# Strassen's seven products for the down projection, with the output projection moved to the last sections

## The chip, the core and the metric

The kernel runs on one core of one Trainium2 chip. The metric is the device time of one execution in microseconds (us), as the median of several runs. The engines are called as in the profile: PE is TensorE (PEld its weight loads), DVE VectorE, ACT ScalarE, POOL GpSimd, SP SyncE, which issues all the DMAs here.

## The reference

One transformer block over 2048 tokens of width 576: attention with 32 heads of width 18, and a gated feed-forward of width 4608 that does not add to it but gates it.

```python
def _A_ref(x, wqkv, wo):
    qkv = (x @ wqkv).reshape(B, S, 3, H, Dh).transpose(2, 0, 3, 1, 4)
    q, k, v = qkv[0], qkv[1], qkv[2]
    scores = jnp.einsum("bhqd,bhkd->bhqk", q, k) * (Dh ** -0.5)
    p = _softmax(scores, axis=-1)
    o = jnp.einsum("bhqk,bhkd->bhqd", p, v)
    return o.transpose(0, 2, 1, 3).reshape(B, S, D) @ wo

def _B_ref(x, w_gate, w_up, w_down):
    return (_gelu(x @ w_gate) * (x @ w_up)) @ w_down

x = A_x
xn = _layernorm(x, axis=-1)
s = _A_ref(xn, A_wqkv, A_wo)
g = _silu(_B_ref(xn, B_w_gate, B_w_up, B_w_down))
return x + s * g
```

All inputs and the output are float32.

## The kernel before

**Precision.** TensorE's operands are in float32r, and every operand is split into a high part (`h`, the value rounded to float32r) and a low part (`l`, the remainder). A product is three matmuls: high by high, high by low, low by high. So each operand made on the chip costs a copy that rounds and a subtraction. For weights and activations POOL does both (`split`, L95), in the lead-in ACT and POOL, in the last sections ACT and DVE (`split_av`).

**Prologue.** Layer norm, transposes and the q, k, v projections run first, and leave q and k (`qk`), v (`vs`) and the transposed tokens (`xhs`) in DRAM.

**Sections.** The rest is a line of 144 feed-forward sections. A section is one block `b` of 512 tokens (four of them) by 128 rows of the width 4608: 27 pairs of matmuls, gate on one half of the array's rows and up on the other (`gate_up`, L387). 36 sections make a block. Two sections (g = 0 and g = 1, even and odd) make a round `r`, 18 rounds to a block. Each section loads the weights of the next and splits them on POOL in three pieces (`wh`, `wl`, five buffers each). Its end is the activation (`activate`, L411): ACT and DVE in turns, six instructions of 512 elements.

**The down product** of a round (`down`, L428) multiplies the two halves of 128 rows that the round made, 512 tokens by 256, with 256 rows of `w_down`, 256 by 576: four blocks of 128 tokens, each 12 matmuls of 288 columns, 48 in all. DVE adds each block to `Y` in SBUF. It runs at the end of the section after the round, an even one, so every second section carries one. The rows of `w_down` are loaded and split again in each of the four blocks.

**Attention** is woven into the 128 sections from the tenth on, four to a unit of 512 queries by four heads. A section has 16 specials spread over its pairs (`spread`, L57), in turn a pair of scores (`score_pair`, whose exponential is on ACT) and a pair for the maxima of the next unit (`max_pair`, whose reduction is on DVE). After the pairs come the products with the values (`values`, L745), then, every fourth section, `max_end` (L716): the maxima of a unit are transposed on TensorE, copied by DVE and stored as rows of that unit's queries; then tasks such as the output projection, then the down product. The nine sections ahead of attention are the lead-in, with maxima alone; seven sections follow it.

**PSUM.** Scores, maxima, values, down and output products share one ring of three buffers (`ring`, L383). Whoever takes a buffer waits until the third user before it has been read.

**The output projection** of the first three blocks is done one group of 128 tokens and 288 columns at a time (14 matmuls), one in every second section of the block after; the last block's groups follow in the last sections.

**Order.** TensorE runs in the order in which the program is written. The other engines' queues are ordered by a scheduler, apart from what `keep_in_program_order` holds fast. Each engine takes its own queue in order.

## Time and profile before

| what | us |
|---|---|
| median of three runs | 2622.2 |
| the three runs | 2620.28 to 2622.35 |
| the profiled execution, its own time | 2619.38 |
| its span in the trace | 2617.6 |

The profile is one execution. The page gives the busy time of each engine, the span in 40 slices, the chain of waits that ended last, and the groups of instructions by line; the trace answers further questions: the chain in order of time, a timeline of each engine, and windows with the busy time of each engine in a stretch. Matmuls are pipelined, so that one lasts longer in the rows than the distance to the next; the chain counts the distance. The clock granted to TensorE was full throughout (1.00).

### The profile page before, as it was taken

The page shows a single profiled execution, that of the slowest core. Times are in us where ns is not written, and L with a number is a line of the kernel's source. Part 1 is how long each engine was busy: PE and PEld are TensorE (multiplying, and loading weights), DVE is VectorE, ACT ScalarE, POOL GpSimd, SP SyncE. Part 2 cuts the span into 40 slices and gives each one's busy share as a digit, 9 for nine tenths or more (in the row PEclk, how much of TensorE's full clock was granted, in tenths as well). Part 3 has the DMA queues.
Part 4 walks back from the last instruction along what each step waited for, and adds up shares of the span by engine and source line. Part 5 has one row for each costly group of instructions (what it writes and reads, how often), then busy time and mean ns, then how long its engine had stood idle before and what let it go on. Part 6 is the DMA issues. An engine that isn't in the chain of part 4 may idle for free.

```text
span 2617.6 us, 54490 instructions
## 1 busy us (share of the span) xinstructions
PE 2592.6 (99%) x20982; PEld 1908.5 (73%) x20982; DVE 1923.2 (73%) x2205; ACT 1400.2 (53%) x1675; POOL 1386.9 (53%) x1507
## 2 busy tenths in 40 slices
PE   9999999999999999999999999999999999999999
PEld 8888766777677666777667677777677777767678
DVE  5326888777887878777787877778887777787445
ACT  3223466555566556555566655555665655565642
POOL 2127554555465455555546555555455755555553
PEclk9999999999999999999999999999999999999999
DMA  8876444434355344444445444445345543544342
GB/s 261 264 241 158 115 104 105 105 93 105 102 132 138 100 108 108 127 113 125 108 112 143 113 125 105 123 107 137 101 111 121 140 112 102 137 108 130 77 115 63
DMA packets 394881, 326.81 MB, mean 125 GB/s; under 512 B 107964, under 2 KB 308668, under 8 KB 394624
## 3 DMA queue, kind: packets, MB, share of 16 engines
q1 hardware_dynamic: 394624, 323.32, 46.4%
q8 instruction: 168, 2.75, 0.5%
q14 instruction: 89, 0.73, 0.1%
HBM read 269.79 MB, written 52.88 MB: 123 GB/s over the span
## 4 chain that ended last, share of the span: by engine, by line
PE 94%; DVE 4%; ACT 1%; issue 0%; DMA 0%; POOL 0%; SPq 0%; POOLq 0%; ACTq 0%
PE pg L401 26%; PE py L435 18%; PE acc L754 14%; PE pe L737 9%; PE pm L705 9%; PE pu L401 8%; PE po L168 7%; PE po L591 2%; DVE mx L706 1%; DVE t L422 1%; PE pgu L401 1%; ACT t L420 1%; DVE m L714 1%; DVE t L415 1%; PE pt L229 0%
## 5 line engine op out<-in xcount | busy, mean ns | idle before, releaser
L738 ACT ACTIVATE pT<-pe 128x1024 f32<-128x1024 f32 x1024 | 1049.5, 1027 | 800.8 <-PE pe L737 771.2
L706 DVE TENSOR_REDUCE mx<-pm 128x2 f32<-128x1024 f32 x1024 | 1217.4, 1226 | 170.0 <-PE pm L705 158.0
L401 PE MATMUL pu<-xd,wh 64*128 64x512 f32 x2520 | 919.7, 395 | 0.0
L401 PE MATMUL pg<-xd,wh 64*128 64x512 f32 x2520 | 918.8, 395 | 0.0
L96 POOL TENSOR_SCALAR wh<-raw 128x384 fp32r<-128x384 f32 x432 | 227.5, 528 | 638.9 <-DMA raw<-in_B_w_up_dram 268.2
L401 PEld LDWEIGHTS pg<-xd,wh 64*128 64x128 f32 x2520 | 464.3, 184 | 92.3 <-issue 22.6
L401 PE MATMUL pg<-xd,wl 64*128 64x512 f32 x1260 | 490.8, 390 | 0.9 <-POOL wl L98 0.9
L401 PE MATMUL pu<-xd,wl 64*128 64x512 f32 x1260 | 491.0, 390 | 0.0
L401 PEld LDWEIGHTS pu<-xd,wh 64*128 64x128 f32 x2520 | 464.3, 184 | 11.1
L754 PE MATMUL acc<-pT,VS 128*32 128x512 f32 x4096 | 466.0, 595 | 0.0
L98 POOL TENSOR_TENSOR wl<-raw,wh 128x384 fp32r<-128x384 f32 x432 | 441.2, 1022 | 33.5
L737 PE MATMUL pe<-q,KS 64*128 64x512 f32 x2048 | 413.5, 392 | 0.0
L705 PE MATMUL pm<-KS,q 64*128 64x512 f32 x2048 | 411.4, 389 | 0.0
L441 DVE TENSOR_TENSOR Y<-py,Y 128x576 f32<-128x576 f32 x272 | 206.0, 758 | 226.7 <-PE py L435 226.3
L435 PE MATMUL py<-dh,hh 128*128 128x288 f32 x1152 | 345.9, 300 | 0.0
L435 PE MATMUL py<-dl,hh 128*128 128x288 f32 x1152 | 339.7, 295 | 0.9 <-POOL dl L103 0.9
L435 PE MATMUL py<-dh,hl 128*128 128x288 f32 x1152 | 339.8, 295 | 0.0
L754 PEld LDWEIGHTS acc<-pT,VS 128*32 128x32 f32 x4096 | 120.4, 109 | 275.4 <-issue 229.5
L737 PEld LDWEIGHTS pe<-q,KS 64*128 64x128 f32 x2048 | 192.3, 184 | 110.9 <-DVE mx L706 29.6
L401 PEld LDWEIGHTS pg<-xd,wl 64*128 64x128 f32 x1260 | 232.3, 184 | 34.3 <-POOL wl L98 1.2
L435 PEld LDWEIGHTS py<-dh,hh 128*128 128x128 f32 x1152 | 216.4, 188 | 39.3 <-issue 37.6
L401 PEld LDWEIGHTS pu<-xd,wl 64*128 64x128 f32 x1260 | 232.3, 184 | 7.1
(138 smaller groups left out, 2989.4 us busy)
## 6 DMA issues: line engine op xcount, KB each, us to landing
KS<-qk SPq DMA_DIRECT2D x1536, 36.0 KB
raw<-in_B_w_gate_dram SPq DMA_DIRECT2D x144, 288.0 KB
raw<-in_B_w_up_dram SPq DMA_DIRECT2D x144, 288.0 KB
raw<-in_B_w_down_dram SPq DMA_DIRECT2D x68, 576.0 KB
VS<-vs SPq DMA_DIRECT2D x128, 152.0 KB
qk<-t SPq DMA_DIRECT2D x72, 256.0 KB
q<-qk SPq DMA_DIRECT2D x384, 36.0 KB
xd<-xhs SPq DMA_DIRECT2D x24, 384.0 KB
```

The lines of the kernel that those rows point to most:

```text
L96: first = nc.gpsimd.tensor_scalar(hi, raw, 1.0, 1.0, op0=ALU.mult, op1=ALU.mult)
L98: keep(nc.gpsimd.tensor_tensor(lo, raw, f(hi), op=ALU.subtract))
L168: nc.tensor.matmul(o, st, m, start=(i == 0), stop=(i == len(terms) - 1))
L401: nc.tensor.matmul(o, w[1 + wp][k][rr, c, :], xd[xp][k][rr, c, :], start=(i == 0), stop=(i == len(terms) - 1))
L435: nc.tensor.matmul(py[:, c, 0:288], h[:, tt], w[:, g, 288 * c:288 * c + 288], start=n == 0, stop=n == len(terms) - 1)
L441: nc.vector.tensor_tensor(yy, py[:, :, 0:288], yy, op=ALU.add)
L591: nc.tensor.matmul(po[:, 0:288], o[x][:, k, :], ow[w][:, k, :], start=(m == 0), stop=(m == len(terms) - 1))
L705: nc.tensor.matmul(pm[:, a], QS[u, r][rr, t * P:(t + 1) * P], KS[(u * NA + c) % KB][r][rr, :], start=True, stop=True)
L706: nc.vector.tensor_reduce(MX[u][:, 2 * r:2 * r + 2, t, c], pm, axis=AX.X, op=ALU.max)
L737: nc.tensor.matmul(pe[:, a], KS[(u * NA + c) % KB][r][rr, t * P:(t + 1) * P], QS[u, r][rr, :], start=True, stop=True)
L738: nc.scalar.activation(PT[u, kt][:, 2 * r:2 * r + 2, :], pe, AF.Exp, scale=SCALE)
L754: nc.tensor.matmul(ACC[u][32 * a:32 * a + 32, :], VS[(u * NA + c) % VB][:, v:v + 32], pt[:, a, :], start=first, stop=last, skip_group_chec ...
```

## The change

It changes three things.

1. The down product of a round, a matrix of 2 by 2 blocks of 256 tokens by 128 rows times one of 128 rows by 288 columns, is done with Strassen's seven products. The seven left factors are the four activations' quarters or sums of two of them (`sums_a`), the seven right factors are sums of quarters of `w_down` (`sums_b`). The products are added up over the rounds in `M`, and combined into the four quarters of the result once at the end of a block (`combine`). The right factors, split, are made once, in block 0, and stored in DRAM (`ts`); in the blocks 1 to 3 `load_t` loads them, 16 KB a partition. `T`, `M` and the left factors `ah`, `al` have one buffer each.
2. The output projection leaves the attention sections. In the seven last sections all 16 groups of 128 tokens are projected, 576 columns each; its weights, heads and reciprocals are loaded there. Its tiles lie in the pool that takes over attention's memory.
3. `max_end` moves from the end of its section into the pairs of the next, behind the fifth special.

The splits change hands: `cut` copies on ACT and subtracts on POOL in the attention sections, on DVE in the lead-in and the last sections.

```diff
+PRODUCTS = ((2, (0, 6)), (5, (1, 3)), (3, (2, 5)), (6, (3, 4)), (0, (4, 2)), (4, (5, 1)), (1, (6, 0)))
+    ts = dram.tile([NR, P, 2 * 7 * DC], F32, name="ts")
...
+    def cut(hi, lo, raw, eng):
+        nc.scalar.activation(hi, raw, AF.Copy)
+        eng.tensor_tensor(lo, raw, f(hi), op=ALU.subtract)
+
+    def sums_a(g, h, eng):
+        ah, al = FF["A"]
+        if g == 0:
+            FF["h0"] = h
+            nc.gpsimd.tensor_tensor(h[:, 2], h[:, 1], h[:, 0], op=ALU.subtract)
+            cut(ah[:, 0:2], al[:, 0:2], h[:, 0:3:2], eng)
+        else:
+            h0 = FF.pop("h0")
+            nc.gpsimd.tensor_tensor(h[:, 4:6], h0[:, 0:2], h[:, 0:2], op=ALU.add)
+            nc.gpsimd.tensor_tensor(h[:, 3], h0[:, 0], h[:, 1], op=ALU.add)
+            nc.gpsimd.tensor_tensor(h[:, 2], h[:, 0], h[:, 1], op=ALU.subtract)
+            cut(ah[:, 2:7], al[:, 2:7], h[:, 1:6], eng)
+
+    def load_t(r):
+        nc.sync.dma_start(f(FF["T"]).rearrange("p i m d -> p (i m d)"), ts[r])
+
+    def sums_b(r, raw, eng):
+        q = raw.rearrange("p g (c d) -> p (g c) d", c=2)
+        t, T = ffn.tile([P, 5, DC], F32, name="tsum"), FF["T"]
+        eng.tensor_tensor(t[:, 1:3], q[:, 0:4:2], q[:, 1:4:2], op=ALU.add)
+        eng.tensor_tensor(t[:, 3:5], q[:, 0:2], q[:, 2:4], op=ALU.subtract)
+        eng.tensor_tensor(t[:, 0], q[:, 0], q[:, 3], op=ALU.add)
+        cut(T[:, 0, 0:2], T[:, 1, 0:2], q[:, 0:4:3], eng)
+        cut(T[:, 0, 2:7], T[:, 1, 2:7], t, eng)
+        nc.sync.dma_start(ts[r], f(T).rearrange("p i m d -> p (i m d)"))
+
+    def down(b, r):
+        (ah, al), T, M = FF["A"], FF["T"], FF["M"]
+        for m, (i, k) in PRODUCTS:
             py = ring("py")
-            for c in range(2):
-                for n, (h, w, g) in enumerate(terms):
-                    nc.tensor.matmul(py[:, c, 0:288], h[:, tt], w[:, g, 288 * c:288 * c + 288],
-                                     start=n == 0, stop=n == len(terms) - 1)
...
+            for t in range(2):
+                tt = slice(t * P, (t + 1) * P)
+                for n, (h, w) in enumerate(((ah, 0), (ah, 1), (al, 0))):
+                    nc.tensor.matmul(py[:, t, 0:DC], h[:, i, tt], T[:, w, k], start=n == 0, stop=n == 2)
             if r == 0:
-                nc.scalar.activation(yy, py[:, :, 0:288], AF.Copy)
+                nc.scalar.activation(M[:, m], py[:, :, 0:DC], AF.Copy)
             else:
-                nc.vector.tensor_tensor(yy, py[:, :, 0:288], yy, op=ALU.add)
+                nc.vector.tensor_tensor(M[:, m], py[:, :, 0:DC], M[:, m], op=ALU.add)
...
+    def combine(one, two):
+        M = FF["M"]
+        one.tensor_tensor(M[:, 6], M[:, 6], M[:, 0], op=ALU.add)
...
+        two.tensor_tensor(M[:, 1], M[:, 1], M[:, 3], op=ALU.subtract)
 
     def gates():
+        for b in FF["gates"]:
+            M = FF["M"]
+            combine(nc.vector, nc.gpsimd)
...
+                tc.keep_in_program_order(nc.scalar.activation(th, y, AF.Tanh, scale=0.25))
+                nc.gpsimd.tensor_scalar(th, th, 1.0, 1.0, op0=ALU.add, op1=ALU.mult)
+                nc.gpsimd.tensor_tensor(th, th, y, op=ALU.mult)
...
+        if g == 0:
+            if b == 0:
+                sums_b(r, FF["rawd"], eng)
+            else:
+                load_t(r)
+        sums_a(g, FF["act"], eng)
...
+            pairs = [p for s in range(s0, s0 + SLOTS) for p in slot_pairs(s)]
+            if ended is not None:
+                pairs.insert(5, lambda: max_end(ended))
+            section(pairs, slots=True)
...
-            if im == 0 and um <= NU:
-                max_end(um - 1)
-            tasks(n, 1)
             downs()
...
+        load_wo()
+        load_o(0)
+        load_xy(*groups[0])
+        split_o(*groups[0])
+        n = 0
+        for i in range(ends):
+            section([], "ring" if i % 2 else "f")
+            if i in (1, 3, 4):
+                load_o({1: 1, 3: 2, 4: 3}[i])
+            downs()
+            finish(nc.vector)
+            while n < cuts[i + 1]:
...
+                project_o(*groups[n])
+                n += 1
```

The new kernel's lines have other numbers: the exponential of the scores is L645 (L738 before), the activation's instructions are L416 to L424, `cut`'s copy is L432 and its subtraction L433, the activation's sums are L440 and L444 to L446, the weights' sums L456 to L458, the weight splits L100 and L102, the copy of the values' sums L665.

The queue of ACT at the end of an odd section (g = 1) in attention, first before. `t` are the activation's tiles, `accs` the copy of the values' sums, `pT` the exponential of the next section's scores `pe`; the brackets name the queues that an instruction waits for.

```order
L414 ACTIVATE t_21847<-pg 128x512 [waits PE_49,Pool_49]
L418 ACTIVATE t_21850<-pu 128x512 [waits DVE_49,PE_49]
L420 ACTIVATE t_21847<-t_21847 128x512 [waits DVE_49]
L758 ACTIVATE accs<-acc 128x512 [waits DMAHW5_49,PE_49]
L738 ACTIVATE pT<-pe 128x1024 [waits PE_49,Activation_49]
L738 ACTIVATE pT<-pe 128x1024 [waits PE_49]
```

The same place in the changed kernel, where `h` is the activation's result with its sums and `ah` the rounded copy of it:

```order
L416 ACTIVATE t_16047<-pg 128x512 [waits PE_49]
L420 ACTIVATE t_16050<-pu 128x512 [waits PE_49]
L422 ACTIVATE t_16047<-t_16047 128x512 [waits DVE_49]
L665 ACTIVATE accs<-acc 128x512 [waits DMAHW5_49,PE_49]
L432 ACTIVATE ah<-h_16046 128x1280 [waits DVE_49,Pool_49]
L645 ACTIVATE pT<-pe 128x1024 [waits PE_49,Activation_49]
L645 ACTIVATE pT<-pe 128x1024 [waits PE_49]
```

A copy of 1280 elements that waits for DVE and POOL now stands between the activation and the next section's first exponential.

The queue of POOL at the end of an odd section, before: two weight splits (`wh`, `wl`), then the split of the activation `t` into `hh` and `hl`.

```order
L96 TENSOR_SCALAR wh<-raw 128x384 [waits DMAHW6_49,DMAHW4_49,PE_49]
L98 TENSOR_TENSOR wl<-raw,wh 128x384 [waits Pool_49]
L96 TENSOR_SCALAR wh<-raw 128x384 [waits PE_49]
L98 TENSOR_TENSOR wl<-raw,wh 128x384 [waits Pool_49]
L96 TENSOR_SCALAR hh<-t_25711 128x512 [waits DVE_49]
L98 TENSOR_TENSOR hl<-t_25711,hh 128x512 [waits Pool_49]
```

The same place in the changed kernel, in block 0, where the weights' sums `tsum` are formed too:

```order
L100 TENSOR_SCALAR wh<-raw 128x384 [waits DMAHW7_49,DMAHW0_49,PE_49]
L102 TENSOR_TENSOR wl<-raw,wh 128x384 [waits Pool_49]
L456 TENSOR_TENSOR tsum<-raw 128x576 [waits DMAHW1_49]
L457 TENSOR_TENSOR tsum<-raw 128x576
L458 TENSOR_TENSOR tsum<-raw 128x288
L100 TENSOR_SCALAR wh<-raw 128x384 [waits PE_49]
L102 TENSOR_TENSOR wl<-raw,wh 128x384 [waits Pool_49]
L444 TENSOR_TENSOR h_7981<-h_7733,h_7981 128x512 [waits DVE_49]
L445 TENSOR_TENSOR h_7981<-h_7733,h_7981 128x256
L446 TENSOR_TENSOR h_7981<-h_7981 128x256
L433 TENSOR_TENSOR al<-h_7981,ah 128x1280 [waits Activation_49]
```

In the blocks 1 to 3 the three rows of `tsum` are missing and the rest is alike. The subtraction `al` now waits for ACT, and the three sums stand ahead of it in the place of `hh` and `hl`.

## The prediction

> **What bounds the kernel now.** I read the page first: the span, the engines' busy time and the chain of waits.

> ```profile
> span 2617.6 us, 54490 instructions
> PE 2592.6 (99%) x20982; PEld 1908.5 (73%) x20982; DVE 1923.2 (73%) x2205; ACT 1400.2 (53%) x1675; POOL 1386.9 (53%) x1507
> PE 94%; DVE 4%; ACT 1%; issue 0%; DMA 0%; POOL 0%; SPq 0%; POOLq 0%; ACTq 0%
> ```

> TensorE sets the time: 94% of the chain is its own work, so the kernel is a stream of matmuls with hardly a gap. An edit pays if it shortens that stream, and costs whatever makes the stream wait. To price both I need one round in the middle of attention, first from the chain, in order of time (start, length, what):

> ```profile
> 1210.64 3.57 PE acc L754 x32
> 1214.21 0.43 PE pg L401
> 1224.32 3.57 PE acc L754 x32
> 1227.89 2.06 PE po L591 x14
> 1229.95 6.37 PE py L435 x48
> ```

> A section is its gate/up pairs with scores and maxima between them (1214.21 to 1224.32, about 10 us), then the values (3.57). Every second section also has the down product, 48 matmuls in 6.37 us, 0.133 us each. The odd sections (g = 1) have none: after the values of 1210.64 the next section's pairs start at once, at 1214.21. The engines beside TensorE at that boundary, from the timeline (start, length, engine, line, idle before it):

> ```profile
> 1210.45 1.23 DVE L706 TENSOR_REDUCE mx<-pm 128x2 f32<-128x1024 f32 x1 [0.16 <-PE pm L705]
> 1212.97 0.69 DVE L422 SCALAR_TENSOR_TENSOR t<-t,t 128x512 f32<-128x512 f32 x1
> 1212.30 0.63 ACT L420 ACTIVATE t<-t 128x512 f32<-128x512 f32 x1 [0.50 <-DVE t L415]
> 1214.28 0.60 ACT L758 ACTIVATE accs<-acc 128x512 f32<-128x512 f32 x1 [1.34 <-PE acc L754]
> 1214.97 2.12 ACT L738 ACTIVATE pT<-pe 128x1024 f32<-128x1024 f32 x2
> 1211.44 0.51 POOL L96 TENSOR_SCALAR wh<-raw 128x384 fp32r<-128x384 f32 x1
> 1213.75 0.62 POOL L96 TENSOR_SCALAR hh<-t 128x512 fp32r<-128x512 f32 x1 [0.70 <-DVE t L422]
> 1214.14 0.50 PE L401 MATMUL pg<-xd,wh 64*128 64x512 f32 x1
> 1216.32 0.39 PE L705 MATMUL pm<-KS,q 64*128 64x512 f32 x2
> ```

> The gated activation is ready at 1213.66 (1212.97 + 0.69), and POOL, idle for 0.70 us, splits it from 1213.75 on. Nobody on ACT waits for that: ACT starts the next section's exponentials at 1214.97. The pair of maxima at 1216.32 is the fourth user of the three-buffer PSUM ring in its section (scores, maxima, scores, maxima), so it needs the buffer of the first scores back, and gets it from the first exponential, 1214.97 + 1.03 = 1216.0. There are 0.3 us of slack.

> The costs of single operations, from the groups by line (count | busy us, mean ns | idle before):

> ```profile
> L738 ACT ACTIVATE pT<-pe 128x1024 f32<-128x1024 f32 x1024 | 1049.5, 1027 | 800.8 <-PE pe L737 771.2 <-PE pu L401 0.4
> L706 DVE TENSOR_REDUCE mx<-pm 128x2 f32<-128x1024 f32 x1024 | 1217.4, 1226 | 170.0 <-PE pm L705 158.0
> L441 DVE TENSOR_TENSOR Y<-py,Y 128x576 f32<-128x576 f32 x272 | 206.0, 758 | 226.7 <-PE py L435 226.3
> L98 POOL TENSOR_TENSOR dl<-raw,dh 128x1152 fp32r<-128x1152 f32 x64 | 171.7, 2683 | 5.1
> L98 POOL TENSOR_TENSOR hl<-t,hh 128x512 fp32r<-128x512 f32 x128 | 165.3, 1291 | 10.4
> L96 POOL TENSOR_SCALAR hh<-t 128x512 fp32r<-128x512 f32 x128 | 79.1, 618 | 86.4 <-DVE t L422 71.9 <-DVE m L713 13.2 <-PE py L435 1.0
> L461 POOL TENSOR_TENSOR th<-th,Y 128x288 f32<-128x288 f32 x24 | 18.9, 808 | 0.0
> L460 POOL TENSOR_SCALAR th<-th 128x288 f32<-128x288 f32 x24 | 9.9, 431 | 0.0
> L102 ACT ACTIVATE dh<-pT 128x1152 fp32r<-128x1152 f32 x4 | 4.6, 1153 | 0.0
> L107 DVE TENSOR_TENSOR dl<-raw,dh 128x1152 fp32r<-128x1152 f32 x4 | 6.4, 1592 | 1.4 <-ACT dh L106 1.4
> L719 PE MATMUL pt<-identr,m 128*32 128x128 f32 x32 | 7.2, 224 | 16.3 <-DVE m L714 16.3
> ```

> **The change part by part.** The sum is made against the profiled execution's span, 2617.6.

> Down product: 7 products of 6 matmuls are 42 instead of 48 of the same shape, so 5.57 us for 6.37, 0.80 less. VectorE now adds seven times per round instead of four: 7 x 0.758 = 5.3 us against 5.57 of TensorE, so it just keeps up, and the ring's three buffers cover the hand-overs; were each hand-over to cost 0.1 us more, 0.3 of the 0.8 would be gone. I take 0.80 for the 68 rounds outside the lead-in: -54.4 us.

> Maxima product: the wait of 16.3 us and the 7.2 of the 32 products become a product and a VectorE copy inside the pairs. There eight reductions of 1.226 already fill the 10 us, so the copy shows; 0.45 us each, 14 in all. -9 us (between 0 and -16).

> Cut of the activation's sums: the heart of the forecast. Before, POOL alone split each half. Now POOL forms three sums of the second half and the first (512, 256 and 256 elements), then ACT copies all five (1280 elements, L432) and only then POOL subtracts. The order of the queues shows that ACT's copy stands ahead of the next section's first exponential. ACT takes its queue in order, so that exponential waits for POOL. Worked through with the boundary above: the half is ready at 1213.66, POOL starts at 1213.75; 1.29 for 512 elements (its row has the same size) and 0.72 twice for 256 (from 808 ns for 288) end at 1216.48. ACT's copy, at 1.0 ns an element by the 1152-element row, takes 1.28; with two hand-overs of 0.09 (1213.66 to 1213.75) it ends at 1217.85, the first exponential at 1218.88, and the maxima pair can start at 1218.97 instead of 1216.32. TensorE loses 2.65 us. It isn't won back: the section's eight slots take 1.23 us each, and VectorE's reduction 1.226. Bounds: 2.0, if POOL's short sums overlap, and 3.2, if the three sums run at POOL's dearest rate (808 / 288 = 2.8 ns). At the even sections the same copy is harmless, since the down product of 5.57 us lies between. Attention has 64 such odd boundaries, 51 without further load: +135 us.

> [...]

> Block 0 forms the weights' combinations. In attention that is 13 rounds, on POOL, and by the order the three sums (576, 576, 288 elements; 1.34 + 1.34 + 0.8 = 3.5 us by 2683 ns for 1152 and by 808 for 288) stand between two weight splits just ahead of the activation's sums. POOL has 0.70 us to spare there (the row at 1213.75; on average 86.4 / 128 = 0.67), so ACT's copy comes 2.8 us later still: 13 x (2.65 + 2.8) = +71 us. Bounds: 13 x 2.65 = 34 if POOL starts early, 110 if the raw buffers, now asked for by three loads in every two sections with the combinations last to release theirs, come another 3 us later.

> Lead-in: VectorE makes all the sums there. The view of the windows over one pair of its sections (length, PE, PEld, DVE, ACT, POOL):

> ```profile
> 241.91:264.15 22.24, 22.24 (x181) 18.64 (x182) 20.45 (x23) 5.76 (x9) 17.35 (x20) 1.00 0.71 180
> ```

> VectorE is at 20.45 of 22.24 us. It gets three more additions (2.3), the weights' sums and cuts (3456 elements at 1.38 ns by 1592 for 1152: 4.8) and the activations' cuts (1792: 2.5). That makes 30, 8 to 9 us over; three pairs have the full maxima: +28 (10 to 35).

> Block ends: POOL gets four multiply-and-adds (0.75 each) and four products (1.45 each, both by the 288-element rows) interleaved with the activation's sums, 8.8 us. ACT there has two exponentials ahead of the copy, worth 2.5 us of cover: 6.3 more, three times, 19. VectorE's four additions over M (0.78 each) fall into a phase without slack: 9. Together +28 (0 to 45).

> Combinations from DRAM: 128 x 16 KB are 2.06 MB for each of 54 rounds, instead of 0.59 MB of raw weights.

> ```profile
> DMA  8876444434355344444445444445345543544342
> GB/s 261 264 241 158 115 104 105 105 93 105 102 132 138 100 108 108 127 113 125 108 112 143 113 125 105 123 107 137 101 111 121 140 112 102 137 108 130 77 115 63
> ```

> The engines are 4 to 5 tenths busy at about 115 GB/s and reached 264. The load may start when the down product is over and is needed some 30 us later; in that time it asks for 70 GB/s more. On SP's queue the load waits for the down product, and keys, values and weights are queued behind it; by the order they are those of one to six sections later. It fits: 0. Without that cover a wait at each of the 54 rounds would come, a rival below.

> Output projection: the same 448 matmuls, moved. 24 x 14 of them (2.06 us each time) leave the attention sections and come back at the end, so TensorE's sum is unchanged. What is late there, with the chain's last rows and the busiest window of the end:

> ```profile
> 2550.00:2560.00 10.00, 10.00 (x83) 8.23 (x79) 5.46 (x7) 2.92 (x4) 9.68 (x12) 1.00 1.08 282
> 2534.13 6.39 PE pgu L401 x54
> 2606.38 7.47 PE po L591 x56
> 2613.88 0.47 DVE thl L895
> L726 SPq DMA_DIRECT2D q<-mr x256: 572/573/732, 282.0 to 2454.0; - x128
> ```

> The new tiles lie where attention's were, so weights of wo (2.8 MB), the first block's heads and reciprocals (2.4), x and gate (0.6) and the combinations (2.1) come only after it, 7.9 MB, 28 us at 282 GB/s (their 33 issues at 0.57 us on SP, the last row, take 19 and lie inside), and 2 us of splits. TensorE has 6.39 + 6.39 + 5.57 = 18 us of other work: +12. At the very end the quarters must be combined after the last down product (POOL 4 x 1.45, then eight additions of 0.8, about 12 us, against 7.47 of projection, which was the only work left before): +5. Together +17 (5 to 40).

> Sum: 2617.6 - 54.4 - 9 + 135 + 71 + 28 + 28 + 17 = 2833. The median of the runs shown, 2622.2, is 4.6 above the span: 2838; I say 2835.

> **Rivals.** (1) The gain comes through. If the sums and the copy were done by the time the first scores are (1214.97), the 135, 71 and 19 fall away: 2617.6 - 54.4 - 9 + 28 + 9 + 17 + 4.6 = 2613, and 2559 if lead-in, block ends and tail hide too. For it speaks TensorE's 94%; against it that 2.7 us of POOL and 1.28 of ACT do not fit between 1213.66 and 1214.97, by rows of equal operations. [...]

> (2) Half a stall: POOL's sums are quicker than their neighbours, or the copy's tail overlaps the exponential. At 1.3 us on 64 boundaries and half of block 0's extra: 2617.6 - 54.4 - 9 + 83 + 18 + 28 + 14 + 17 + 4.6 = 2719.

> (3) The combinations come late. The load starts behind the down product and shares the one queue with keys, values and weights. It decides once it takes over 30 us, less than 70 GB/s of its own; the free half of the engines' 264 speaks against it. Each us late costs 54: at 3 us, 2835 + 162 = 2997.

> **How the numbers follow.** The forecast 0.70 with its own range 2690 to 2920 (the terms' lower and upper bounds, not all at once); half a stall 0.14; the gain comes through 0.11; late combinations 0.05. The range must reach into the second case: 2670 to 2920. A measurement of this kernel tells about 0.2% (5 us) from no change: of case 1, 0.09 is faster and 0.02 within; the rest is slower, 0.89.

> **What would show it.** In the profile after, the first exponential of every even section idle behind L432, with POOL's L446 as its releaser; TensorE idle 2 to 3 us at the second maxima pair, twice that in block 0; a round in blocks 1 to 3 about 1.9 us longer than before without its projection; the down product at 5.6 us for 42 matmuls; no wait for T. If TensorE stays above 97% busy, the cut doesn't block ACT and I am wrong in the main term; if VectorE's additions pace the down product above 5.8 us, in the first.

## The result and the profile after

The changed kernel takes 3143.66 us (median of 4 runs, 3139.48 to 3144.13) against 2621.55 for the kernel before (4 runs, 2620.28 to 2622.35): 1.1989 times as long, 95% interval 1.1968 to 1.2009. The forecast of slower came out, its size did not: 2835 was predicted, 2920 was the end of the range. The page of the profile after, engines, slices of the span and the chain of waits:

```profile
span 3142.3 us, 53942 instructions
...
PE 2715.6 (86%) x20550; PEld 1965.3 (63%) x20550; DVE 2166.6 (69%) x2467; ACT 1551.6 (49%) x1843; POOL 1448.4 (46%) x1493
...
PE   9987777768768899999998899999997899999767
...
PEclk9998889889888999999999999999998999999889
...
PE 64%; POOL 11%; DMA 8%; DVE 7%; issue 4%; ACT 3%; SPq 2%; POOLq 0%; DVEq 0%; ACTq 0%
```

TensorE has 432 instructions fewer and is still busy 123 us longer; PEclk says why: its granted clock, full throughout before, is under 90% in 11 of the 40 slices and 0.924 on average. The low state is half clock (below), so 0.076 x 3142 x 2 = 478 us were spent in it. TensorE was also idle 427 us, 25 before. In the stretches at half clock it was idle for 189 us; the other 290 us of work, by an estimate from the ratio of the granted clocks (0.50 to 1.00), would have taken half of that at full clock. So of the 525 us some 402 are idle time and, by this estimate, some 145 the slower clock, less 57 for the 432 matmuls; about 35 us of busy time stay unexplained.

To find where the 525 us lie I took the start of each of the 144 sections (its first ScalarE instruction, the square of the gate, L416) in each kernel and summed by stretch. "Ends" are the five sections from the last of a block on, "regular" the others of blocks 1 to 3 in attention, "last sections" the time from section 135 to the end of the span; ahead of the lead-in lie 203 to 205 us in each kernel. Each row is one profiled execution; that of e3_max_back was its fastest, 13 us under its median. The kernels below the change are the experiments. The predicted column is the prediction's terms, sorted by stretch (64 odd boundaries: 13 in block 0, 9 at ends, 41 regular, 1 after; the 44.6 us of 24 moved projections, 1.86 each by the section starts, leave the regular stretch for the last one).

| us | lead-in | block 0 | 3 ends | regular | last sections |
|---|---|---|---|---|---|
| before | 96.5 | 445.9 | 258.5 | 1500.9 | 111.6 |
| predicted | 124.5 | 506.5 | 303 | 1523 | 172 |
| after | 150.0 | 616.7 | 351.9 | 1585.5 | 234.5 |
| e3_max_back | 149.6 | 610.5 | 336.7 | 1523.4 | 229.8 |
| e1_late_copy | 149.3 | 533.4 | 311.5 | 1444.3 | 235.0 |
| f2_parts | 157.7 | 514.0 | 300.0 | 1444.6 | 238.1 |
| h2_store_only | 140.4 | 488.5 | 310.5 | 1444.6 | 235.6 |
| h1_store_behind | 139.0 | 458.9 | 296.5 | 1444.6 | 198.7 |
| p1_left_out | 114.7 | 459.7 | 280.0 | 1444.1 | 195.6 |

Every stretch is longer than predicted, by 25 to 110 us. The groups by line of the changed kernel (count | busy us, mean ns | idle before, releaser) first, since the main term was built on them:

```profile
L444 POOL TENSOR_TENSOR h<-h,h 128x512 f32<-128x512 f32 x72 | 93.5, 1298 | 103.2 <-DVE h L424 54.5 <-DVE m L620 27.6 <-DVE h L427 21.1
...
L432 ACT ACTIVATE ah<-h 128x1280 fp32r<-128x1280 f32 x72 | 91.4, 1269 | 368.1 <-POOL h L446 368.1
...
L445 POOL TENSOR_TENSOR h<-h,h 128x256 f32<-128x256 f32 x72 | 54.4, 756 | 0.0
L446 POOL TENSOR_TENSOR h<-h 128x256 f32<-128x256 f32 x72 | 52.9, 735 | 0.0
...
L474 DVE TENSOR_TENSOR M<-py,M 128x576 f32<-128x576 f32 x476 | 358.7, 756 | 34.3 <-PE py L470 19.7
```

The operations cost what was priced (1298, 756, 735 and 1269 ns for 1290, 720, 720 and 1280), and ScalarE's copy waits 368 us, all of it for GpSimd's third sum: the mechanism is there. What the operations set off was not priced. One regular boundary, from the timeline:

```profile
1261.87 0.75 POOL L446 TENSOR_TENSOR h<-h 128x256 f32<-128x256 f32 x1
...
1262.65 1.27 ACT L432 ACTIVATE ah<-h 128x1280 fp32r<-128x1280 f32 x1 [1.63 <-POOL h L446]
...
1263.83 1.92 ACT L645 ACTIVATE pT<-pe 128x1024 f32<-128x1024 f32 x2
...
1264.89 0.57 PE L612 MATMUL pm<-KS,q 64*128 64x512 f32 x2 [2.24 <-ACT pT L645]
```

TensorE stands for 2.24 us at the second maxima pair. But the interval from the odd section to the even one is 17.84 us where it was 13.70 (with the maxima product 18.59 and 14.4), 4.14 more. The view of the windows around this stall and around another one of the same length in the same block (length, PE, PEld, DVE, ACT, POOL busy, granted clock, DMA share, GB/s) shows the rest:

```profile
1187.09:1190.51 3.42, 1.65 (x16) 1.07 (x12) 1.23 (x1) 1.80 (x3) 2.04 (x4) 1.00 0.42 108
1190.51:1193.92 3.41, 2.96 (x26) 2.70 (x26) 2.35 (x3) 2.85 (x4) 3.33 (x3) 1.00 0.80 176
1262.19:1265.60 3.41, 1.17 (x10) 0.74 (x10) 0.71 (x2) 2.95 (x3) 2.03 (x2) 1.00 0.58 159
1265.60:1269.01 3.41, 3.41 (x20) 3.41 (x18) 2.34 (x2) 1.51 (x3) 2.83 (x3) 0.50 0.44 97
1269.01:1272.43 3.42, 3.42 (x33) 3.11 (x32) 2.90 (x3) 2.73 (x3) 0.84 (x2) 1.00 0.66 159
```

After the second stall TensorE works 3.41 us at half clock, 20 matmuls instead of 33; after the first it does not, and that interval is 16.29. The window edges are no free choice. The clock dropped 72 times, at 1115.42, 1152.96, 1228.06, 1265.60 and so on, and all the distances are whole multiples of 3.4133 us within 0.3% of one. The regular stretch has 41 boundaries, 39 without the last two, whose sections have no maxima; 35 of these 39 have a drop. Laid on this grid, each of the 35 stalls has at least 1.99 us of idle in one window (2.24 in the row of 1262.19), and the four without a drop at most 1.87: their idle time lies on both sides of an edge (1.77 and 0.45 in the first two rows).

The idle time ahead of a drop is not always one piece. In the lead-in a window of the same grid holds two waits of TensorE, 1.11 and 0.87 us with work between them, and the clock drops behind it:

```profile
272.33:275.74 3.41, 1.43 (x10) 0.86 (x10) 3.41 (x3) 0.15 (x1) 0.00 (x0) 1.00 0.00 0
275.74:279.15 3.41, 3.01 (x14) 2.42 (x16) 3.41 (x4) 0.00 (x0) 0.00 (x0) 0.50 1.11 454
```

### The profile page after: what moved, and what is told of

Same layout as the page of the kernel before. It is cut to its first block, busy times and chain, and to the rows that moved or that the text cites. A ratio compares the mean times of both kernels' runs of the same rounds, so it can differ in the third digit from the quotient of the medians.

```text
span 3142.3 us, 53942 instructions
## 1 busy us (share of the span) xinstructions
PE 2715.6 (86%) x20550; PEld 1965.3 (63%) x20550; DVE 2166.6 (69%) x2467; ACT 1551.6 (49%) x1843; POOL 1448.4 (46%) x1493
## 4 chain that ended last, share of the span: by engine, by line
PE 64%; POOL 11%; DMA 8%; DVE 7%; issue 4%; ACT 3%; SPq 2%; POOLq 0%; DVEq 0%; ACTq 0%
PE pg L406 17%; PE py L470 12%; PE acc L661 8%; PE pm L612 7%; PE pe L644 7%; PE pu L406 6%; PE po L172 6%; POOL h L444 3%; DMA raw<-in_B_w_up_dram 2%; DVE mx L613 2%; ACT pT L645 2%; DMA raw<-in_B_w_down_dram 2%; POOL h L446 1%; POOL h L445 1%; POOL T L433 1%
## 5 line engine op out<-in xcount | busy, mean ns | idle before, releaser
L645 ACT ACTIVATE pT<-pe 128x1024 f32<-128x1024 f32 x1024 | 1038.9, 1025 | 501.0 <-PE pe L644 480.4
L406 PE MATMUL pg<-xd,wh 64*128 64x512 f32 x2520 | 981.0, 421 | 11.8 <-POOL wh L100 8.7
L406 PE MATMUL pu<-xd,wh 64*128 64x512 f32 x2520 | 980.8, 421 | 4.8 <-DVE t L421 2.7
L612 PE MATMUL pm<-KS,q 64*128 64x512 f32 x2048 | 454.5, 422 | 312.3 <-ACT pT L645 288.7
L100 POOL TENSOR_SCALAR wh<-raw 128x384 fp32r<-128x384 f32 x432 | 227.6, 528 | 977.3 <-PE pu L406 652.4
L612 PEld LDWEIGHTS pm<-KS,q 64*128 64x128 f32 x2048 | 225.6, 200 | 383.2 <-ACT pT L645 329.1
L102 POOL TENSOR_TENSOR wl<-raw,wh 128x384 fp32r<-128x384 f32 x432 | 445.3, 1032 | 32.8
L470 PE MATMUL py<-T,ah 128*128 128x288 f32 x2016 | 418.5, 303 | 24.1 <-DVE M L474 23.4
L432 ACT ACTIVATE ah<-h 128x512 fp32r<-128x512 f32 (+1 forms) x144 | 137.1, 952 | 578.7 <-POOL h L446 368.1
L474 DVE TENSOR_TENSOR M<-py,M 128x576 f32<-128x576 f32 x476 | 358.7, 756 | 34.3 <-PE py L470 19.7
L470 PEld LDWEIGHTS py<-T,ah 128*128 128x128 f32 x2016 | 326.0, 191 | 83.9 <-issue 56.8
L433 POOL TENSOR_TENSOR al<-h,ah 128x1280 fp32r<-128x1280 f32 (+1 forms) x128 | 269.1, 2102 | 206.2 <-ACT ah L432 203.7
L470 PE MATMUL py<-T,al 128*128 128x288 f32 x1008 | 299.3, 297 | 0.0
```

Of the source, the lines that this page charges most:

```text
L100: first = nc.gpsimd.tensor_scalar(hi, raw, 1.0, 1.0, op0=ALU.mult, op1=ALU.mult)
L102: keep(nc.gpsimd.tensor_tensor(lo, raw, f(hi), op=ALU.subtract))
L406: nc.tensor.matmul(o, w[1 + wp][k][rr, c, :], xd[xp][k][rr, c, :], start=(i == 0), stop=(i == len(terms) - 1))
L433: eng.tensor_tensor(lo, raw, f(hi), op=ALU.subtract)
L470: nc.tensor.matmul(py[:, t, 0:DC], h[:, i, tt], T[:, w, k], start=n == 0, stop=n == 2)
L474: nc.vector.tensor_tensor(M[:, m], py[:, :, 0:DC], M[:, m], op=ALU.add)
```

## The experiments

**The copy out of the queue.** In attention the copy and the subtraction of an odd section wait until the fifth exponential of the next one.

```diff
-            cut(ah[:, 2:7], al[:, 2:7], h[:, 1:6], eng)
+            if late:
+                FF["late"] = lambda: cut(ah[:, 2:7], al[:, 2:7], h[:, 1:6], eng, tc.keep_in_program_order)
+            else:
+                cut(ah[:, 2:7], al[:, 2:7], h[:, 1:6], eng)
...
+            if "late" in FF:
+                pairs.insert(9, FF.pop("late"))
             section(pairs, slots=True)
```

> The changed kernel with one edit: in attention ScalarE's copy of the odd section's five activation sums (and GpSimd's subtraction behind it) is issued behind the fifth exponential of the next section instead of ahead of its first. Theory A (the copy blocks ScalarE's queue, and the stall of 2.8 us then also halves TensorE's granted clock for some 3.4 us): the odd-to-even interval of blocks 1 to 3 returns from 17.85 to about 13.8 us, the granted clock there to 1.00, and with half of block 0's and of the block ends' excess the time falls from 3143 to about 2850 us. Theory B (the prediction's own: the queue costs 2.65 us and the slower clock has another cause): the interval falls to about 15.2 us and the time to about 2970. Theory C (the stall comes from the down product's sums or from the combinations' load): no change beyond 10 us.

Measured: 2875.06 us (2 runs; 1.0965 times before, 1.094 to 1.099). The odd-to-even interval is 14.13 without the product and 15.08 with it, the granted clock rises from 0.924 to 0.963, and the groups by line show the copy's wait cut to a third:

```profile
L432 ACT ACTIVATE ah<-h 128x1280 fp32r<-128x1280 f32 x72 | 91.3, 1267 | 121.6 <-POOL h L446 121.6
```

Theory A. The regular stretch loses 141 us for 41 boundaries, 3.44 each; the prediction had 2.65. By its trace no clock drop is left in that stretch (35 in the change), and over the whole kernel the mean of 0.963 leaves 213 us at half clock of 479. Some 0.4 us of each boundary stay (0.7 with the product), and no run here says why.

**Shorter chains.**

```diff
-            nc.gpsimd.tensor_tensor(h[:, 3], h0[:, 0], h[:, 1], op=ALU.add)
-            nc.gpsimd.tensor_tensor(h[:, 2], h[:, 0], h[:, 1], op=ALU.subtract)
+            blk = (FF["n"] - 1) // (NR * G)
+            (nc.vector if blk == 3 else nc.gpsimd).tensor_tensor(h[:, 3], h0[:, 0], h[:, 1], op=ALU.add)
+            (nc.vector if blk >= 2 else nc.gpsimd).tensor_tensor(h[:, 2], h[:, 0], h[:, 1], op=ALU.subtract)
```

> The changed kernel with GpSimd's chain ahead of the copy shortened by block: block 1 as it is, in block 2 one of the two short sums on VectorE, in block 3 both. GpSimd's chain before the copy is then 2.79, 2.05 and 1.30 us, so the bare stall should be about 2.8, 2.0 and 1.3 us. Theory A (a stall under some length leaves the clock at 1.00, so the cost falls by more than the stall): odd-to-even intervals of 17.85, about 15.7 and 15.0 us, the granted clock beside the boundary 1.00 in block 3, the whole about 3070 us. Theory B (cost in proportion to the stall, 1.5 us for each us): 17.85, 16.7 and 15.6 us, the whole about 3095.

Measured: 3115.67 us (one run). Both theories miss, and the doses came out smaller than meant: by the trace the copy starts 2.79 us behind the activation's end in block 1, 2.33 in block 2 and 1.99 in block 3, so of the 0.74 and 1.49 us that GpSimd is spared, 0.3 and 0.7 come back with the sums on VectorE. In block 2 the interval without the product is 17.86 (17.84 in block 1), with it 18.1 (18.6), and all 15 regular stalls still drop the clock; why the 0.46 us gain nothing without the product stays open. In block 3 seven of nine don't drop it, and their intervals are 15.96 to 16.42. In this run windows with 1.49 to 1.78 us of idle, 44 to 52% of 3.41, stand on both sides (1.49 with a drop behind it, 1.78 without), so no sharp bound shows.

**The maxima product back at its section's end.**

```diff
-            if ended is not None:
-                pairs.insert(5, lambda: max_end(ended))
...
             load_v(n + 2)
+            if im == 0 and um <= NU:
+                max_end(um - 1)
```

> The changed kernel with one part undone: the maxima product is back at the end of its section, as before the change. The prediction's term says that the move gains 9 us, so 3152 us here. The rival, from the intervals of the changed kernel (18.6 us with the product, 17.85 without, as large a difference as the old kernel's 14.4 to 13.7): the move gains nothing, 3143 plus or minus 4.

Measured: 3069.45 us (5 runs; 1.1706 times before, 1.1684 to 1.1728), 74 us faster than the change (88 in the profiled execution, 62 of them in the regular stretch). I had expected at most 4 either way, and the prediction 9 the other way. In the trace nearly all regular intervals are 16.28, with the product and without, and the clock drops at 3 of 39 stalls. So the theory had to explain why the same stall no longer costs a half clock. Two things differ. Where the product stands, it now breaks TensorE's idle time in two pieces of 1.0 and 0.84 us. From the start of the first to the end of the second it is 4.5 us, more than the 3.41 of a window: the window of 1209.11 holds 1.08 us of idle, that of 1212.52 holds 0.84, and the clock stays at 1.00 behind both:

```profile
1211.97 0.22 PE L626 MATMUL pt<-identr,m 128*32 128x128 f32 x1 [1.01 <-DVE m L621]
...
1215.45 0.57 PE L612 MATMUL pm<-KS,q 64*128 64x512 f32 x2 [0.84 <-ACT pT L645]
```

And between two stalls without the product lie 71.57 us, 20.97 windows, so that their place on the grid hardly moves and they go on straddling an edge, with at most 1.63 us of idle in one window where no drop follows. In the change it is 75.1 us, 22 windows: with the half clock in it, two rounds are a whole number of windows, and the next stall falls where the last one did.

**The same with no stall, and the move alone on the kernel before.** The first is the late copy and the product moved back together. The second puts the edits of the move, the lines just shown with their signs turned round, into the kernel before.

> e1_late_copy with the maxima product back at the end of its section as well. Undoing the move alone had gained 74 us, all of it in odd-to-even intervals that shrank from 17.85 and 18.6 to 16.28, with the same stall of some 2.2 us but without the half clock. Theory A (the clock is decided on a fixed grid of 3.41 us, the distance of the drops, and the move only shifted the stalls on it): with the stalls gone by the late copy the same undoing is worth little, at most the 0.3 us by which the intervals with the product stand out more than before the change, so 2875 minus 0 to 10 us. Theory B (the moved product itself costs 2 us at each boundary): about 2800.

> The kernel before with one part of the change alone: the maxima product moved into the next section's pairs. The prediction's term says 9 us faster (0 to 16): 2613. The rival, by the intervals of the changed kernel (0.75 to 0.95 us more with the product inside, as much as with it outside): no gain, 2622 plus or minus 5.

Measured: 2876.81 (4 runs, 1.0978, 1.0963 to 1.0993) against 2875.06 for the late copy alone; and 2620.26 (11 runs; 0.9997, 0.9988 to 1.0006). In neither kernel does the product's place change the whole. In the first this is a balance: by the section starts the old place costs 9 us in the regular stretch (15.37 for 15.08 in the intervals with the product) and gains 7 in block 0 and 4 at the ends. So the bulk of the 74 us was the clock's, as the 32 drops that are gone at the regular stalls say: at 1.56 us each they make 50.

**A shift on the grid.** One more pair of matmuls in each odd section, overwritten by the first real pair.

```diff
+        def twice():
+            for a, o in enumerate((pg, pu)):
+                rr = slice(HR * a, HR * a + HR)
+                nc.tensor.matmul(o, w[1][0][rr, 0, :], xd[0][0][rr, 0, :], start=True, stop=True)
...
+        if n in ATT and n % G:
+            first = todo[0]
+            todo[0] = lambda: (twice(), first())
```

> e3_max_back (3069 us, no half clock at its regular boundaries) with one more pair of gate and up matmuls, 0.42 us of TensorE, in each of the 64 odd sections; the extra pair is overwritten by the section's own first pair and changes nothing but the time. Theory A (TensorE's clock is decided by the idle share of each window of a fixed grid of 3.41 us: in the changed kernel all 41 drops of the regular boundaries lie on one grid, and e3's stalls of the same length just straddle its edges): the shift makes some to most stalls fall inside one window again, so that part of the odd-to-even intervals is 16.7 and part about 18.3, and the time grows by more than the added work, to 3110 to 3160 us. Theory B (e3 was faster because the moved product costs time in itself): every interval is 16.7 us, and the time is 3069 + 64 x 0.42 = 3096 us or less.

Measured: 3080.22 us (4 runs; 1.175, 1.1722 to 1.1778), and here I missed: the pair costs 0.23 us, not 0.42, and only two more stalls drop the clock (5 of 39). The intervals do split as theory A has it, into 16.28 and 17.85, and each stall keeps to the bound (2.01 us of idle in a window or more with a drop, at most 1.83 without). But the stalls broken by the product never drop it, and the others move by only 0.1 window from one to the next; I had counted on every stall. The grid explains which stalls drop the clock; I could not forecast how many.

**The load of the combinations.**

```diff
-        nc.sync.dma_start(f(FF["T"]).rearrange("p i m d -> p (i m d)"), ts[r])
+        nc.sync.dma_start(f(FF["T"]).rearrange("p i m d -> p (i m d)")[:, 0:DC], ts[r][:, 0:DC])
```

> The changed kernel with the load of the combinations from DRAM in blocks 1 to 3 cut to 288 of its 4032 columns, so that the down products of those blocks use the stale rest (the output is another). If these 2.06 MB a round come late or hold up the keys, values and weights behind them on the queue (the prediction's third rival), the time falls by 20 us or more. If they are hidden, as priced in the prediction, it stays within 6 us of 3143 in blocks 1 to 3; the last sections, whose queue is full, may give another 10 to 20.

Measured: 3126.99 us (4 runs; 1.1924, 1.1908 to 1.1941). Block 0 and the regular stretch stay within 1.4 us of the change (616.9 and 1586.9); 9 us are gained in the last sections and 11 at the ends, where I had not looked for any. The 2.06 MB are hidden in the regular stretch, as priced.

**Block 0, and other stretches by the way.** Four edits on the late copy: an own buffer for the rows of w_down; in the lead-in all cuts on GpSimd; the gate's products as one VectorE instruction each; the reciprocals' loads on ScalarE's queue. To make room, the activation's scratch tile `t1` has one buffer instead of two here and in every kernel below with the own buffer. A second kernel adds the product's old place and another order of the last loads (the second diff below, where the weights' loads are also held in program order).

```diff
-            section(pairs, slots=True)
+            section(pairs, raw_d=lambda: att.tile([P, G, D], F32, name="rawd"), slots=True)
...
-            finish(nc.vector)
+            finish()
...
-                nc.gpsimd.tensor_scalar(th, th, 1.0, 1.0, op0=ALU.add, op1=ALU.mult)
-                nc.gpsimd.tensor_tensor(th, th, y, op=ALU.mult)
+                nc.vector.scalar_tensor_tensor(th, th, 1.0, y, op0=ALU.add, op1=ALU.mult)
...
-                    keep(nc.sync.dma_start(den[rows], rT[h:h + m, toks].rearrange("h (o s) -> h o s", o=1)
+                    keep(nc.scalar.dma_start(den[rows], rT[h:h + m, toks].rearrange("h (o s) -> h o s", o=1)
```

```diff
-            if i in (1, 3, 4):
-                load_o({1: 1, 3: 2, 4: 3}[i])
             downs()
             finish(nc.vector)
+            if i in (1, 3, 4):
+                load_o({1: 1, 3: 2, 4: 3}[i])
```

> e1_late_copy with four edits in four separate stretches, each read from the section starts. Block 0 in attention (533 us in e1): the rows of w_down get a buffer of their own; if the two shared raw buffers hold the loads up, it falls to about 470, and if GpSimd's own work is the bound it stays above 515. Lead-in (149 us): weights' sums and all cuts on GpSimd instead of VectorE; if VectorE bounds it as the prediction has it, about 125; if the weight splits on GpSimd come too late by it, above 155. Block ends (excess of about 20 us each): the gate's eight products on VectorE as four, which frees GpSimd of 8.8 us; about 12 each if GpSimd holds them up, no change if the loads of the next block's x do. Last sections (234 us): the reciprocals' loads on ScalarE's queue, which halves the issues that stand on SP's queue ahead of the weights; about 200 if the issues bound them, above 225 if the bytes do. All together about 2740.

> f2_parts with two more edits: the maxima product back at its section's end, and in the last sections the weights' and the combinations' loads issued ahead of the next block's heads. If the order on SP's queue is what the last sections wait for, they fall by another 15 us or more; if it is the splits and products, by less than 5. The whole about 20 us under f2_parts; still slower than the kernel before, since lead-in, block ends and last sections keep more than the 54 us that the products save.

Measured: 2861.12 us (one run) and 2883.04 us (4 runs; 1.0988, 1.0964 to 1.1012), 120 us above what I expected for the first and 20 above the first instead of under it for the second. Block 0 gains 19 us, the ends 12; lead-in (158) and last sections (238 and 257) get longer. So the lead-in does not gain by GpSimd either, and neither the number of issues on SP nor this order is what the last sections wait for. The trace of f2_parts shows what block 0 waits for. GpSimd's waits there (in all, times, longest):

```profile
POOL tsum L459 <- DMA rawd<-in_B_w_down_dram: 90.2, 11, 9.1
```

And from its timeline two rows of SP's queue and two of GpSimd:

```profile
629.56 0.35 SPq L464 DMA_DIRECT2D ts<-T  x1
629.95 0.43 SPq L520 DMA_DIRECT2D rawd<-in_B_w_down_dram  x1
...
628.09 1.44 POOL L433 TENSOR_TENSOR T<-rawd,T 128x576 fp32r<-128x576 f32 x1
639.22 1.44 POOL L459 TENSOR_TENSOR tsum<-rawd 128x576 f32<-128x576 f32 x1 [8.11 <-DMA rawd<-in_B_w_down_dram]
```

GpSimd's cut of round r, done at 629.53, lets go both the store of the combinations (2.06 MB) and the load of the next rows (0.59 MB). The store is issued first, the load lands 9.3 us later behind it, and GpSimd holds the next weights' sums, and behind them the activation's, until then.

**The store behind the load.** Both are built on the late copy. The first kernel has the own buffer too, the gate's products on VectorE, the weights' sums of the lead-in on GpSimd, and leaves out the reciprocals' loads but for 128 rows; the second has the store's new place alone and the heads' normalisation on GpSimd (last line below).

```diff
-        nc.sync.dma_start(ts[r], f(T).rearrange("p i m d -> p (i m d)"))
+        FF["store"] = lambda: tc.keep_in_program_order(nc.sync.dma_start(ts[r], f(T).rearrange("p i m d -> p (i m d)")))
...
             nc.sync.dma_start(raw, w_down[r * G * P:(r + 1) * G * P, :].rearrange("(g p) n -> p g n", p=P))
+        if g == 0 and "store" in FF:
+            FF.pop("store")()
...
-                den = DN[b, k] = epi.tile([P, TB], F32, name="den", bufs=2)
+                den = DN[b, k] = DN[0, 0] if DN else epi.tile([P, TB], F32, name="den")
...
+                    if b == 0 and k == 0:
...
-                nc.vector.tensor_tensor(o[0:n, k, :], o[0:n, k, :], den[0:n], op=ALU.mult)
+                nc.gpsimd.tensor_tensor(o[0:n, k, :], o[0:n, k, :], den[0:n], op=ALU.mult)
```

> e1_late_copy with edits in separate stretches. Block 0 (533 us in e1, 514 in f2_parts, where the rows of w_down had their own buffer but their load landed 9 us after its issue, behind the 2.06 MB store of the combinations that was issued just ahead of it): own buffer, and the store is queued behind the next rows' load. If that store is the cause of GpSimd's 8 us wait in each round, block 0 falls to about 450 to 470; if GpSimd's own work is, it stays above 500. Lead-in (149 us): the same store no longer heads SP's queue while its cut is made, and the weights' sums go to GpSimd, the activations' cuts stay on VectorE; about 125 if the queue and VectorE were the bound, no change if the total of work is. Block ends: the gate's products on VectorE, as in f2_parts. Last sections (234 us): the reciprocals' loads are left out but for the first 128 rows (the output is another); if VectorE's normalisations, that wait for these loads at the head of its queue, hold up the additions and the activations behind them, about 190; if not, above 225.

> e1_late_copy with only the store of the combinations queued behind the next rows' load, the two raw buffers shared as in the change, and, in the last sections, the normalisation of the heads on GpSimd. Block 0: about 470 if the store's place is the cause and two buffers do, above 510 if the third user of the two buffers is the cause. Lead-in: about 135 if the store at the head of SP's queue was what held up the weights, 149 if VectorE's sums are the bound. Last sections: below 215 if only VectorE's queue was held up by the reciprocals' loads, 230 or more if the wait just moves to GpSimd's weight splits.

Measured: 2745.76 us (2 runs; 1.0472, 1.0427 to 1.0518) and 2823.65 (2 runs; 1.0769, 1.0725 to 1.0814). Block 0 is 458.9 with both and 488.5 with the store alone, from 533.4: the store's place is 45 us, and the own buffer behind it 30 (alone, in f2_parts, it was 19). Lead-in 139 and 140: the store's place gives 9 us. Last sections 199 without the reciprocals' loads, 236 with the normalisation on GpSimd. The waits of VectorE in the change and of GpSimd in h2_store_only, over the last sections (in all, times, longest):

```profile
DVE OT L781 <- DMA den<-rT: 38.9, 10, 12.0
```

```profile
POOL OT L788 <- DMA den<-rT: 51.7, 14, 7.7
```

In both kernels the engine that normalises waits for these loads at the head of its queue (38.9 and 51.7 us), with VectorE's additions or GpSimd's weight splits behind it. Whether the 36 us come from these waits or from the bytes of the loads was not separated.

**The rest, by leaving out.** First, on h2_store_only with the normalisation back on VectorE, the lead-in's weights' combinations on VectorE; then, on h1_store_behind, these and the activations' subtraction, the combinations and gate at the ends, and the heads' and reciprocals' loads of all blocks but the first.

```diff
+        if eng is nc.vector:
+            for i in range(2):
+                for a, n in ((0, 2), (2, 4), (6, 1)):
+                    nc.scalar.activation(T[:, i, a:a + n], q[:, 0:n], AF.Copy)
...
-            combine(nc.vector, nc.gpsimd)
...
+            if b:
+                OT[b] = OT[0]
+                return
```

> e1_late_copy with the store of the combinations queued behind the next rows' load, as in h2_store_only (lead-in 140 us there, 96.5 before the change), and in the lead-in's five rounds VectorE's part of the weights' combinations left out (three sums and the two subtractions, by the trace 8 us a round; ScalarE copies raw rows in their place, so the output is another). If VectorE's load is what makes the lead-in long, as the prediction has it, it falls by at least half of these 40 us, to 120 or less; if the wait is for loads, splits and queues, it stays above 130.

> h1_store_behind with more left out, stretch by stretch (the output is another). Lead-in: the weights' combinations are left out as in l1_lead_none (125 us there), and the activations' subtraction runs on GpSimd, so that VectorE keeps only what it had before the change and three additions a round. If VectorE's load is the rest, about 105; if it is ScalarE's copy behind GpSimd's three sums, in the chain to each down product, it stays above 120. Block ends (297 us): the combinations of the products and the gate's multiplications are left out. If they hold the ends up, about 275 (the old 258.5 and ten stalls less ten savings); if it is the loads and casts of the next block's x and the restart behind them, above 290. Last sections (199 us): the heads and reciprocals are loaded once, for the first block. If these loads and the normalisations behind them are the rest, about 170 (the old 111.6, 44.6 of projections and 10 of combining at the end make 166); if not, above 190.

Measured: 2812.43 us (one run) and 2700.81 us (2 runs); lead-in 124.9 and 114.7. VectorE's weights' sums and cuts are 15 us (I had asked for 20 to call it the cause), the activations' subtraction 10; 18 of the 53.5 us stay open. Ends 280: combining and gating are 16 us less than in h1_store_behind, beyond the 12 that f2_parts had taken. Last sections 195.6, only 3 less than in h1_store_behind, but two edits stand against each other there: p1_left_out loads all of the first block's reciprocals again, of which h1_store_behind had only 128 rows. The section starts part them. The section in which the first block's heads come in takes 45.1 us in e1_late_copy, 33.8 in h1_store_behind and 44.9 in p1_left_out; the four sections behind it take 112, 87 and 73. So the first block's reciprocals are 11 us and the later blocks' heads and reciprocals 39; without either, by this estimate, 184 would be left, 18 above the expected 166. What those are was not tested.

## Why the prediction was wrong

The direction was right, and so was the mechanism of the stall; the sum lacked what a stall sets off, and four terms were too small.

**Down product: right.** The even-to-odd interval fell from 20.27 to 19.50: 0.77 of the predicted 0.80. VectorE's additions (756 ns) kept up.

**Maxima product: wrong, 0 for 9.** g1_before_max_moved shows nothing gained: its intervals with the product are 14.45 us, 14.4 before. VectorE's copy inside full pairs seems to cost what the wait of 16.3 us did. With the stalls of the change the move cost 74 us, for a reason that was not in the prediction.

**Cut of the activation's sums: the step "TensorE loses 2.65 us" lacked its sequel.** The bare stall was right (16.28 - 13.70 = 2.58). What failed is that a stall was priced as time alone: at 35 of 39 regular boundaries the clock halves for 3.41 us behind it, 17.84 - 16.28 = 1.56 more. That is 55 us of the 62 by which the regular stretch missed. No row of the trace before could show it: there TensorE is idle for at most 1.59 us in any 3.41 up to its last matmuls (the wait ahead of 11.13), and the granted clock stays at 1.00. But nothing in the prediction asked what a kernel with stalls of 2.65 us would be granted.

**Block 0: the step "ACT's copy comes 2.8 us later still" was mis-sized; 171 us for 61.** By the trace the copy starts 12.3 us behind the activation's end there and 2.79 in the other blocks, so it comes 9.5 us later still. The odd-to-even interval went from 14.2 to 28.05. GpSimd's three sums are 3.6 us, as priced. The raw buffers were named, as a bound of 3 us; they and the store issued ahead of the load are 75 us over 13 rounds (533.4 to 458.9), 5.7 a round. The copy's place in ScalarE's queue, with the half clock behind its stall, is another 83 (616.7 to 533.4): 12 of the 13 rounds of the change have four windows, 13.65 us, at half clock. The store had been counted on no queue: combinations "from DRAM" were costed by their loads in blocks 1 to 3 alone.

**Lead-in: 53.5 for 28.** VectorE's load was the right cause for half of it (15 + 10), the store on SP's queue for 9; 18 stay open. (Three pairs at 8 to 9 us are 24 to 27; the sum took 28.)

**Block ends: 93 for 45 with their boundaries.** The late copy takes 40, the gate and combinations 12 and 16; 4 lie between f2_parts and h1_store_behind, and 21 stay. What these are was not tried. Cutting the combinations' load alone, in e4_t_small, gave 11 there.

**Last sections: 123 for 60.** The overhang behind the last matmul was right in kind (13.6 us from TensorE's end at 3128.66 against 3.8; +10 for +5). The step "33 issues on SP lie inside" saw the first block only: the later blocks' heads and reciprocals, which the sum had at nothing, are 39 us (p1_left_out), and the first block's reciprocals, which it had counted by their bytes alone, 11 (h1_store_behind).

**Rivals.** Neither the gain nor half a stall came; the third (combinations late in blocks 1 to 3) is excluded by e4_t_small but for 20 us at the ends and in the last sections. The clock, by the estimate above some 145 of the 308 us beyond the forecast, was no rival at all.

No version beat the kernel before. The best that leaves nothing out is h2_store_only (2823.65 us). By an estimate from the table, h1's stretches up to the last and the change's last one make 2778 us, 6% slower; no run has them together.

## What to carry to other kernels

In a kernel whose TensorE hardly ever idles, price a new wait with the slower clock that can follow it: here 3.41 us at 0.50 stood behind 35 of 39 stalls, and what told them from the other four was the idle time within one window, not that of the whole kernel. Look at what an in-order queue holds behind a waiting instruction, on DMA queues too: here the 2.06 MB store of the combinations, let go by the same event as the next load, cost 45 us in block 0 until it stood behind that load (h2_store_only). Where additions on other engines replace multiplications, ask what waits in those engines' queues behind the additions: here 54 us were saved on TensorE and 402 lost to its waits.

## What the hardware showed

At half clock the figures are others: in the change the 67 windows at 0.50 with 0.64 us of idle or more were each followed by another at 0.50, the 71 with 0.59 or less never. That is the picture in block 0: in 12 of its 13 rounds TensorE is idle through the first two of four windows in a row and for 0.92 to 2.95 us of the third, works through the fourth, and all four are at 0.50.

Five runs of e3_max_back spread over 19.6 us (3056.22 to 3075.79), eleven of g1_before_max_moved, without such stalls, over 3.1. Only one run of each has a trace, and what spreads them was not shown.
